# Projection tiles as four matmuls of 512 columns, and 22 steps of zero matmuls placed anew among TensorE's early steps

## The chip, the cores and the metric

One NeuronCore of a Trainium2 chip runs the whole program. The metric is the device time of one execution in microseconds (us); of the kernel before, three runs are shown and their median is the time it is compared by. A profile shows one further execution, instruction by instruction.

## The reference

The program joins two layers. The first is linear attention with exponential features, for 8 batches, 8 heads, 576 tokens and a head width of 64; the second is a gated long convolution over the 576 tokens with a model width of 512, done with Fourier transforms.

```python
def phi(x):                                   # x: (8, 8, 576, 64), w_phi: (64, 128)
    proj = np.einsum('bhsd,df->bhsf', x, w_phi)
    proj = proj - np.max(np.abs(proj), axis=-1, keepdims=True)
    return np.concatenate([np.exp(proj), np.exp(-proj)], axis=-1)
q_p, k_p = phi(q), phi(k)
kv = np.einsum('bhsf,bhsd->bhfd', k_p, v)
z = np.sum(k_p, axis=2)
x = einsum('bhsf,bhfd->bhsd', q_p, kv) / (einsum('bhsf,bhf->bhs', q_p, z)[..., None] + 1e-06)
# the heads side by side: x is (8, 576, 512)
x1, x2, x3 = split(x @ w_proj, 3)             # w_proj: (512, 1536)
x2_conv = irfft(rfft(x2) * rfft(filter))      # along the 576 tokens
out = (x1 * x2_conv * x3) @ w_out             # w_out: (512, 512)
```

## The kernel before

The order of all work is written out by hand. `PLAN` is a string of some 1,500 words; `run` takes them one after the other and calls the method of that name. A word is a step, its arguments, and behind an @ the PSUM bank (one of eight, 512 float32 columns each) in which it works; a method that needs two banks takes the next one too. Each engine executes its own steps in the order of the words; between engines there are only semaphores, which follow from who writes and reads which tile. So a step waits for the last reader of its bank and for its inputs, and everything behind it on its engine waits with it.

The 576 tokens of a batch are cut into nine residues j modulo 9 of 64 tokens. The letter b is a batch (0 to 7), v one of four pairs of heads. The steps that matter here, by engine:

- TensorE: `wz` multiplies a tile of zeros, `zz`, by itself: two matmuls of 512 columns into a bank that nothing reads (line 318). `pt` transposes q or k of batch 0 (line 613). `Qn` and `Pk` make the features of q and k with the tokens on the partitions, to find their largest absolute value (lines 639 and 632); `Qnt` and `Pkt` do so for the last residue (647). `trm` transposes the maxima (736). `Pq` makes the features of q once more, transposed, with the maximum subtracted by a second group of matmuls (666 and 672). `KV` sums k's features times v (765), `NE` multiplies q's features by that (779). `X1`, `X3` are tiles of the projection, made by `proj` (920); `X2` is its middle third, made on Fourier coefficients (898). `F` and `I` are the Fourier transform and its inverse (859, 863 and 973). `O` is the output projection (1020).
- VectorE (DVE in the profile): the reductions `maxq` and `maxk` (line 708), the division `xn` (798), products and copies from PSUM. `mlo` (732) makes the low part of the maxima.
- ScalarE (ACT): all exponentials `ex` (694), the sines of the Fourier tables (458 to 468), copies from PSUM such as `pte` (299).
- GpSimd (POOL): `vs`, which scales v (line 750), `f1` and `f2` (847, 853), and the issue of most loads.
- SyncE (SP): transposes by DMA, `trh` for q and k and `trx` for x (817), and the stores `st` (1029), in one queue.

Four things about the projection are needed. `proj` works on x transposed, `xT`, whose four blocks `kt` of 128 rows come from the four pairs of heads v and so from four separate DMA transposes. Each block holds 4 x 128 tokens, in four groups. The two halves d of the groups go through separate accumulations: for d = 0 four matmuls of 256 columns over kt = 0..3, then for d = 1 four more, which read their columns in reverse. The result is written to the bank in blocks of 128 columns, every other block for one half. There are 32 tiles of `X1` and 32 of `X3`.

Of the kernel before, what the change touches and what calls it, by code (L numbers as in the profile page):

```python
# [31 lines left out]
zeros gi_part fl_load,0,1 gz,DVE cols_i loadh,q,0,0 wz,25@2 w_load,phi loadh,k,0,1 wz,12@6  # L32
loadh,q,0,1 fl_load,3,0 wz,27@2 fl_load,3,1 cols_h gi_nr fl_load,1,1 ident cols_f gi_fr wz,20@3
fl_load,2,1 fl_load,2,0 wz,9@2 ang,2 fl_load,1,0 loadh,k,0,0 wz,10@5 fl_load,0,0 ang,3 wz,1@3
load,q,1 load,k,1 pt,q,0,0,1@7 pt,q,0,0,0@0 frac,2 pte,DVE,q,0,0,1@7 pte,ACT,q,0,0,0@0 frac,3
ang,1 sin,3 pt,k,0,1,0@5 ang,0 pt,k,0,1,1@6 w_phi sin,2 frac,1 Qn,0,0@3 cols_m pte,ACT,k,0,1,0@5
frac,0 sin,1 Pk,0,2@1 pte,DVE,k,0,1,1@6 maxk,0,2@1 pt,q,0,1,0@7 sin,0 Qn,0,1@5 one
pte,DVE,q,0,1,0@7 fa,POOL,1 maxq,0,1@5 pt,k,0,0,0@0 ex,k,p,0,2@1 pte,DVE,k,0,0,0@0 pt,k,0,0,1@5
ex,k,m,0,2@1 maxq,0,0@3 Qn,0,2@6 load,v,0 back,ACT pte,ACT,k,0,0,1@5 Pk,0,0@0 maxq,0,2@6
ex,k,m,0,0@0 trh,q,1,0 zm,POOL Pk,0,1@4 pt,q,0,1,1@3 fa,POOL,0 maxk,0,1@4 ex,k,p,0,0@0 Pk,0,3@6  # L40
trh,q,1,1 pte,ACT,q,0,1,1@3 maxk,0,0@0 ex,k,p,0,3@6 Qn,0,3@2 maxq,0,3@2 ex,k,m,0,3@6 Qnt,0@0
ex,k,p,0,1@4 maxqt,0@0 Pkt,0@2 maxk,0,3@6 mhi,0 rv@0 exkt,m,0@2 rve,ACT,0@0 trh,k,1,0 ex,k,m,0,1@4
mlo,DVE,0 maxkt,0@2 trm,0@6 rve,DVE,1@0 em,m,0,0 em,m,0,1 trme,DVE,0@6 em,p,0,0 vs,POOL,m,0,0
trh,k,1,1 Pqt,0@4 exkt,p,0@2 Qn,1,0@6 Pq,0,1@0 exqt,p,0@4 maxq,1,0@6 exqt,m,0@4 fl_loadt em,p,0,1
ex,q,m,0,1@0 Qn,1,3@6 vs,DVE,p,0,0 load,k,2 Pq,0,2@4 Pq,0,3@2 ex,q,p,0,1@0 w_load,proj,2
maxq,1,3@6 vs,POOL,p,0,1 ex,q,p,0,3@2 Pk,1,1@0 maxk,1,1@0 KV,0,0@6 ex,q,m,0,3@2 ex,q,p,0,2@4
Qnt,1@2 w_load,proj,0 KVe,DVE,0,0@6 ex,q,m,0,2@4 vs,POOL,m,0,1 maxqt,1@2 NE,0,1@6 Qn,1,2@2
ex,k,p,1,1@0 rc,0,1@6 Pq,0,0@4 xn,0,1@6 ft,ACT maxq,1,2@2 trx,0,1 KV,0,1@6 load,v,1 ex,k,m,1,1@0
load,q,2 trh,k,2,0 ex,q,p,0,0@4 Pk,1,0@0 KVe,DVE,0,1@6 w_load,proj,1 maxk,1,0@0 NE,0,2@6
ex,q,m,0,0@4 zl,POOL NE,0,3@2 rc,0,2@6 Pk,1,3@4 ex,k,p,1,0@0 xn,0,2@6 rc,0,3@2 NE,0,0@6  # L50
ex,k,m,1,0@0 xn,0,3@2 rc,0,0@6 NEt,0@2 f1,POOL,0,1,1 ex,k,p,1,3@4 xn,0,0@6 Pkt,1@0 rct,0@2
ptx,0,2@6 xnt,0,1@2 exkt,p,1@0 Hd,4@7 f1,POOL,0,0,0 xnt,0,0@2 exkt,m,1@0 ptxe,DVE,0,2@6 maxk,1,3@4
ptx,0,0@2 f1,POOL,0,1,0 He,ACT,4,0@7 Hd,0@3 ptxe,ACT,0,0@2 Qn,1,1@6 maxkt,1@0 ex,k,m,1,3@4
f1,POOL,0,0,1 Hd,3@2 maxq,1,1@6 Hd,1@0 em,m,1,0 He,ACT,0,0@3 f2,POOL,0,1,1 Pk,1,2@4 em,p,1,0
He,DVE,1,0@0 mhi,1 ptx,0,3@6 ex,k,p,1,2@4 Hd,2@7 f2,POOL,0,1,0 ptxe,DVE,0,3@6 He,DVE,0,1@3
X1,0,3@1 late He,ACT,2,0@7 maxk,1,2@4 f2,POOL,0,0,0 He,ACT,3,1@2 X1,0,2@6 He,ACT,1,1@0 mlo,DVE,1
X1,0,0@7 X1e,DVE,0,3@1 f2,POOL,0,0,1 ex,k,m,1,2@4 He,DVE,3,0@2 trm,1@3 X1e,ACT,0,0@7 trh,q,2,0
vs,DVE,m,1,0 F,0,3@4 load,v,2 trme,ACT,1@3 F,0,1@0 Fe,ACT,0,3@4 X3,0,0@2 X1e,DVE,0,2@6 em,m,1,1
vs,POOL,p,1,0 trh,k,2,1 Fe,ACT,0,1@0 F,0,2@4 tm,0,0@2 F,0,0@6 Fe,ACT,0,2@4 Pq,1,1@0 Fe,ACT,0,0@6
Pk,2,0@2 vs,POOL,m,1,1 KV,1,0@4 ex,q,p,1,1@0 maxk,2,0@2 ex,q,m,1,1@0 X2,0,3@7 KVe,DVE,1,0@4  # L60
em,p,1,1 ex,k,p,2,0@2 X3,0,2@6 vs,POOL,p,1,1 Y1,0,3@7 Xl,ACT,0 X2,0,2@1 trxt,0 ex,k,m,2,0@2
tm,0,2@6 Pk,2,1@4 Y1,0,2@1 trh,q,2,1 X2,0,0@7 load,q,3 ex,k,p,2,1@4 load,k,3 X2,0,1@3 ex,k,m,2,1@4
Y1,0,0@7 w_load,out X1,0,1@2 maxk,2,1@4 m3,POOL,0,1 Pkt,2@0 X1e,ACT,0,1@2 Pq,1,0@6 exkt,m,2@0
Y1,0,1@3 X3,0,3@2 exkt,p,2@0 ex,q,p,1,0@6 X2,0,4@5 load,k,4 maxkt,2@0 m3,POOL,0,0 tm,0,3@2 X1t,0@4
ex,q,m,1,0@6 Qn,2,1@0 Y1,0,4@5 Pq,1,2@2 em,p,2,0 em,m,2,0 maxq,2,1@0 X1te,ACT,0@4 X3t,0@7
ex,q,p,1,2@2 NE,1,1@4 vs,POOL,m,2,0 tmt,0@7 NE,1,0@0 ex,q,m,1,2@2 rc,1,1@4 xn,1,1@4 I,0,0@6
rc,1,0@0 I,0,2@4 xn,1,0@0 Ie,0,0@6 Im,0,0@6 f1,POOL,1,0,0 Pq,1,3@0 Ie,0,2@4 Ip,0,0@6 KV,1,1@2
Ip,0,2@4 ex,q,m,1,3@0 Im,0,2@4 trh,k,3,1 vs,POOL,p,2,0 ex,q,p,1,3@0 Pk,2,2@6 I,0,1@4 maxk,2,2@6
trx,1,1 KVe,ACT,1,1@2 X3,0,1@1 Ie,0,1@4 f1,DVE,1,0,1 ex,k,p,2,2@6 Ip,0,1@4 I,0,3@2 ym,POOL,0,0
Im,0,1@4 tm,0,1@1 NE,1,3@4 Ie,0,3@2 ex,k,m,2,2@6 ym,POOL,0,2 wz,13@0 Ip,0,3@2 NE,1,2@0 rc,1,3@4  # L70
Im,0,3@2 xn,1,3@4 trh,k,3,0 Pqt,1@2 ym,POOL,0,1 Qn,2,0@6 exqt,m,1@2 rc,1,2@0 KV,2,0@4 maxq,2,0@6
exqt,p,1@2 ym,POOL,0,3 trx,1,3 xn,1,2@0 NEt,1@2 KVe,ACT,2,0@4 O,0,3@6 rct,1@2 f2,DVE,1,0,0 trx,1,2
f2,DVE,1,0,1 O,0,0@7 f1,DVE,1,1,1 Oe,ACT,0,3@6 f1,DVE,1,1,0 xnt,1,1@2 Qn,2,3@4 f2,POOL,1,1,1
Qnt,2@0 xnt,1,0@2 O,0,1@6 maxq,2,3@4 O,0,2@3 Oe,ACT,0,1@6 Oe,DVE,0,0@7 F,1,0@4 f2,DVE,1,1,0
Oe,ACT,0,2@3 st,SP,0,0,1 F,1,1@6 maxqt,2@0 Fe,ACT,1,0@4 trh,q,3,1 F,1,3@2 Fe,DVE,1,1@6 F,1,2@0
Fe,ACT,1,3@2 Qn,2,2@4 Fe,ACT,1,2@0 trx,1,0 Pk,2,3@6 maxq,2,2@4 X2,1,1@3 ex,k,m,2,3@6 X2,1,2@0
trh,q,3,0 ex,k,p,2,3@6 Y1,1,1@3 X2,1,3@1 mhi,2 maxk,2,3@6 mlo,POOL,2 trh,k,4,1 load,q,4 trm,2@5
X1,1,3@2 trme,ACT,2@5 load,v,3 Y1,1,2@0 X1,1,2@4 st,SP,0,2,0 X1e,ACT,1,3@2 st,SP,0,3,1 Pq,2,1@2
Y1,1,3@1 X1e,ACT,1,2@4 Qn,3,2@6 em,m,2,1 X1,1,0@4 ex,q,p,2,1@2 maxq,3,2@6 m3,POOL,1,1 X3,1,2@5
ex,q,m,2,1@2 Pq,2,0@0 X1e,ACT,1,0@4 tm,1,2@5 Qn,3,0@6 em,p,2,1 ex,q,p,2,0@0 X3,1,0@3 vs,POOL,m,2,1  # L80
maxq,3,0@6 ex,q,m,2,0@0 NE,2,1@4 tm,1,0@3 Pq,2,2@6 Xl,ACT,1 rc,2,1@4 Pkt,3@0 X3,1,3@2 xn,2,1@4
vs,POOL,p,2,1 exkt,p,3@0 exkt,m,3@0 trx,2,1 NE,2,0@4 ex,q,p,2,2@6 tm,1,3@2 X2,1,0@3 rc,2,0@4
xn,2,0@4 trxt,1 ex,q,m,2,2@6 X1,1,1@2 Y1,1,0@3 f1,POOL,2,0,0 Pqt,2@6 trh,k,4,0 X1e,ACT,1,1@2
KV,2,1@4 maxkt,3@0 exqt,m,2@6 exqt,p,2@6 f1,DVE,2,0,1 Pk,3,1@2 st,SP,0,2,1 KVe,ACT,2,1@4 Pq,2,3@0
f2,POOL,2,0,1 maxk,3,1@2 trx,2,0 NE,2,2@6 ex,q,p,2,3@0 X2,1,4@4 m3,POOL,1,0 rc,2,2@6 ex,q,m,2,3@0
xn,2,2@6 trh,q,4,1 X1t,1@5 Y1,1,4@4 NEt,2@6 X1te,ACT,1@5 NE,2,3@0 ex,k,p,3,1@2 trx,2,2 rct,2@6
f2,POOL,2,0,0 X3,1,1@4 xnt,2,1@6 xnt,2,0@6 ex,k,m,3,1@2 rc,2,3@0 I,1,0@6 xn,2,3@0 tm,1,1@4 X3t,1@5
trx,2,3 f1,POOL,2,1,0 Ie,1,0@6 I,1,2@2 Im,1,0@6 tmt,1@5 f1,POOL,2,1,1 st,SP,0,1,1 Pk,3,0@0
Ip,1,0@6 Ie,1,2@2 Pk,3,2@4 ex,k,m,3,0@0 Ip,1,2@2 I,1,3@6 trh,q,4,0 Im,1,2@2 maxk,3,2@4 wz,14@2
ym,POOL,1,2 Ie,1,3@6 I,1,1@2 trxt,2 Im,1,3@6 ex,k,m,3,2@4 ym,POOL,1,0 Ip,1,3@6 X1,2,2@6 maxk,3,0@0  # L90
st,SP,0,0,0 X1,2,0@7 Ie,1,1@2 ex,k,p,3,2@4 st,SP,0,3,0 ym,POOL,1,3 Im,1,1@2 st,SP,0,1,0 Ip,1,1@2
X1,2,1@2 X1e,ACT,2,2@6 f2,DVE,2,1,0 X1e,ACT,2,0@7 Qn,3,3@3 X3,2,2@6 ym,POOL,1,1 em,p,3,0
maxq,3,3@3 em,m,3,0 ex,k,p,3,0@0 X1t,2@7 vs,POOL,p,3,0 tm,2,2@6 O,1,0@5 yt,ACT,1 X1te,ACT,2@7
X1e,ACT,2,1@2 Qnt,3@6 Pk,3,3@0 Oe,ACT,1,0@5 Qn,3,1@3 maxqt,3@6 ex,k,p,3,3@0 O,1,2@2 st,SP,1,0,1
maxq,3,1@3 load,q,5 F,2,0@5 ex,k,m,3,3@0 f2,POOL,2,1,1 O,1,4@7 Oe,DVE,1,2@2 Fe,ACT,2,0@5
maxk,3,3@0 O,1,3@3 load,k,5 mhi,3 Oe,ACT,1,4@7 mlo,POOL,3 F,2,1@5 load,k,6 em,m,3,1 F,2,3@0
Fe,DVE,2,1@5 vs,POOL,m,3,0 trm,3@7 X3t,2@4 Fe,ACT,2,3@0 X3,2,0@2 trme,ACT,3@7 tmt,2@4 Oe,ACT,1,3@3
F,2,2@0 tm,2,0@2 Qnt,4@4 Fe,ACT,2,2@0 Pq,3,0@6 maxqt,4@4 Qn,4,0@2 em,p,3,1 KV,3,0@0 ex,q,p,3,0@6
vs,POOL,p,3,1 maxq,4,0@2 ex,q,m,3,0@6 X2,2,2@4 KVe,ACT,3,0@0 Pq,3,1@2 vs,POOL,m,3,1 Y1,2,2@4
Pq,3,3@6 ex,q,p,3,1@2 trh,k,5,0 X2,2,3@1 ex,q,m,3,1@2 NE,3,0@4 Y1,2,3@1 load,v,4 st,SP,1,2,1  # L100
X3,2,1@0 ex,q,p,3,3@6 st,SP,1,2,0 rc,3,0@4 Pq,3,2@2 ex,q,m,3,3@6 m3,POOL,2,1 xn,3,0@4 X2,2,0@1
tm,2,1@0 trx,3,0 ex,q,p,3,2@2 NE,3,1@4 Y1,2,0@1 X2,2,1@7 ex,q,m,3,2@2 X1,2,3@6 rc,3,1@4 Xl,DVE,2
xn,3,1@4 Y1,2,1@7 Qn,4,2@2 X1e,ACT,2,3@6 trx,3,1 Pkt,4@0 KV,3,1@4 maxkt,4@0 m3,POOL,2,0 X3,2,3@6
# [982 lines left out]
```

## Time and profile before

| | |
|---|---|
| three runs | 307.57, 308.5, 310.66 us; median 308.5 us |
| the profiled execution | 307.3 us, of which 305.5 us from the first to the last instruction |
| TensorE's mean granted clock in the span | 0.969 |
| TensorE busy | 275.5 us, 4253 matmuls, 4287 weight loads |
| VectorE, ScalarE, GpSimd busy | 262.3, 223.0 and 216.4 us |

In the profile's rows the first number is the start in us from the span's start, the second the time that the row takes, then the engine, the line of the kernel, the operation, what it writes and reads, its shape and how many instructions are merged. The bracket at the end is the idle time of that engine before the row and what ended it. A matmul's length holds its way through the array: matmuls follow one another more closely than their lengths say, so their pitch is read from the starts of two rows.

### The profile page before, as it was taken

The numbers are of one execution on the slowest core, as the hardware profiler recorded it, in microseconds if no ns is written. First come the engines' busy times: TensorE is split into PE (matmuls) and PEld (weight loads), VectorE is DVE, ScalarE is ACT, GpSimd is POOL, SyncE is SP. The second block draws the span as 40 slices with busy tenths as digits, with TensorE's granted clock in tenths as the row PEclk, the third lists the DMA queues.
The fourth block names the chain that finished last, engine by engine and source line by source line (L and its number), as shares of the span: only waits on it lengthen the run. The fifth ranks groups of instructions, "written<-read, shape, count | busy, mean of one in ns | idle before, by whom it ended". The sixth has DMA issues, their size and how long they took to land.

```text
span 305.5 us, 10146 instructions
## 1 busy us (share of the span) xinstructions
PE 275.5 (90%) x4253; PEld 199.7 (65%) x4287; DVE 262.3 (86%) x448; ACT 223.0 (73%) x360; POOL 216.4 (71%) x180
## 2 busy tenths in 40 slices
...
ACT  1998986888359978876987688976757988843240
...
PEclk9855999999999999999999999999999999999998
...
GB/s 144 242 200 133 206 136 179 157 153 191 108 118 187 144 136 134 189 177 144 131 151 154 140 92 177 165 163 102 4 139 65 103 89 10 72 55 60 2 120 190
DMA packets 72734, 40.18 MB, mean 132 GB/s; under 512 B 53040, under 2 KB 67504, under 8 KB 72688
## 3 DMA queue, kind: packets, MB, share of 16 engines
...
q14 instruction: 13, 0.11, 0.1%
HBM read 33.75 MB, written 9.44 MB: 141 GB/s over the span
## 4 chain that ended last, share of the span: by engine, by line
PE 69%; DVE 15%; ACT 5%; DMA 5%; issue 4%; SPq 0%; DVEq 0%
PE ps L920 15%; PE ps L898 9%; PE ps L1020 8%; PE ps L973 6%; PE ps L765 5%; DMA xT<-xn 5%; PE ps L779 3%; DVE mk L708 3%; PE ps L666 3%; PE ps L929 2%; PE ps L672 2%; PE ps L639 2%; PE ps L859 2%; PE ps L318 2%; PE ps L863 2%
## 5 line engine op out<-in xcount | busy, mean ns | idle before, releaser
L920 PE MATMUL ps<-xT,wproj 128*128 128x256 bf16 x512 | 64.2, 273 | 2.3 <-DMA xT<-xn 2.2
L920 PEld LDWEIGHTS <-wproj 128*128 128x128 bf16 x512 | 48.3, 98 | 12.7 <-issue 2.9
L708 DVE TENSOR_REDUCE mk<-ps 128x8 f32<-128x1024 f32 (+1 forms) x40 | 44.2, 1109 | 6.1 <-PE ps L632 5.4
L708 DVE TENSOR_REDUCE mq<-ps 128x8 f32<-128x1024 f32 (+1 forms) x40 | 44.0, 1109 | 5.1 <-PE ps L639 3.6
L912 POOL TENSOR_TENSOR T<-T,T 128x1024 bf16<-128x1024 bf16 x15 | 31.9, 2127 | 18.3 <-DVE T L908 18.2
L1009 POOL TENSOR_TENSOR yT<-cv,x1s 128x576 bf16<-128x576 f32 x27 | 34.3, 1295 | 11.6 <-DVE cv L994 11.5
L750 POOL TENSOR_TENSOR vm<-vn,vm 128x1152 bf16<-128x1152 bf16 x15 | 32.9, 2194 | 9.3 <-ACT vm L744 9.3
L694 ACT ACTIVATE Ekp<-ps 128x1024 bf16<-128x1024 f32 x32 | 33.1, 1033 | 3.9 <-PE ps L632 2.6
L694 ACT ACTIVATE Ekm<-ps 128x1024 bf16<-128x1024 f32 x32 | 33.0, 1032 | 4.0 <-DVE mk L708 2.6
L750 POOL TENSOR_TENSOR vp<-vn,vp 128x1152 bf16<-128x1152 bf16 x15 | 32.2, 2155 | 5.1 <-ACT vp L744 5.1
L694 ACT ACTIVATE Eqp<-ps 128x1024 bf16<-128x1024 f32 x32 | 32.8, 1026 | 3.4 <-PE ps L672 3.2
L1020 PE MATMUL ps<-wout,yT 128*128 128x512 bf16 x130 | 34.0, 380 | 1.2 <-DVE yT L1009 0.4
L694 ACT ACTIVATE Eqm<-ps 128x1024 bf16<-128x1024 f32 x32 | 32.5, 1028 | 3.3 <-PE ps L672 2.5
L847 POOL TENSOR_TENSOR SD<-xn 128x512 bf16<-128x512 bf16 x23 | 26.3, 1160 | 10.1 <-DVE xn L798 8.6
L853 POOL TENSOR_TENSOR xf<-SD 128x512 bf16<-128x512 bf16 x24 | 27.8, 1169 | 7.1 <-DVE SD L847 5.7
L898 PE MATMUL ps<-wproj,XF 128*128 128x512 bf16 x116 | 30.3, 380 | 0.9 <-ACT XF L299 0.2
L973 PE MATMUL ps<-inv,T 128*128 128x288 bf16 x192 | 27.6, 286 | 0.1
L994 DVE TENSOR_TENSOR cv<-es,ps 128x288 f32<-128x288 f32 x64 | 25.6, 443 | 1.4 <-ACT es L991 1.1
L299 ACT CAST x1s<-ps 128x512 bf16<-128x512 f32 (+1 forms) x34 | 17.9, 543 | 11.8 <-PE ps L920 9.9
L961 DVE TENSOR_TENSOR x1s<-ps,x1s 128x512 bf16<-128x512 f32 x32 | 21.7, 684 | 5.0 <-PE ps L920 4.1
L991 ACT COPY es<-ps 128x288 f32<-128x288 f32 x32 | 12.9, 404 | 14.2 <-PE ps L973 13.7
L798 DVE TENSOR_TENSOR xn<-ps,r 128x512 bf16<-128x512 f32 x32 | 22.0, 689 | 0.9
...
## 6 DMA issues: line engine op xcount, KB each, us to landing
...
```

Source lines behind the costliest of these rows:

```text
L694: self.nc.scalar.activation(e, p, AF.Exp, bias=0.0, scale=1.0 if g == "p" else -1.0)
L708: self.nc.vector.tensor_reduce(out=out, in_=src, axis=AX.X, op=ALU.max, apply_absolute_value=True)
L750: self.eng(eng).tensor_tensor(out=t[:, :, :, 0:64], in0=self.at("vn", b)[:, 2 * X:2 * X + 2], in1=t[:, :, :, 64:65].to_broadcast([128, 2, ...
L847: self.eng(eng).tensor_tensor(out=o[:, :, 2 * i:2 * i + 2, :], in0=x[:, :, 0:2, :], in1=x[:, :, 2:4, :], op=ALU.subtract if i else ALU.add)
L853: self.eng(eng).tensor_tensor(out=o[:, :, 2 * i:2 * i + 2, :], in0=x[:, :, 0:4:2, :], in1=x[:, :, 1:4:2, :], op=ALU.subtract if i else ALU ...
L898: self.mm(self.pb(0), l, w[:, kt, 512:1024], start=(kt == 0), stop=(kt == 3))
L912: self.eng(eng).tensor_tensor(out=Y, in0=Y, in1=self.at(f"T{2 * e + 1}", b), op=ALU.add)
L920: self.mm(o[:, d], w[:, kt, f0 + 128 * m:f0 + 128 * m + 128], y[:, 1, ::-1, ::-1] if d else y[:, 0], start=(kt == 0), stop=(kt == 3))
L973: self.mm(self.pb(e, 0, 288), l, inv[:, 2 * e + i if i < 2 else 4 + e, :], start=(i == 0), stop=(i == 2))
L994: self.nc.vector.tensor_tensor(out=self.turn_of("cv", (b, m))[:, :, odd, :], in0=self.turn_of("es", (b, m)).rearrange("p (x t) -> p x t", ...
L1009: self.eng(eng).tensor_tensor(out=self.at("yT", b)[:, m, 0:SEQ], in0=self.turn_of("cv", (b, m)).rearrange("p x h t -> p (x h t)"), in1=sel ...
L1020: self.mm(self.pb(0), y[:, kt, 128 * c:128 * c + 128], w[:, kt, :], start=(kt == 0), stop=(kt == 3))
```

## The change

Three edits belong together. First, `proj` makes a tile with four matmuls of 512 columns, one for each kt, and no longer with two halves. Second, so that the columns stand in the right order without a reversed reading, the token order of two of the four groups is turned at its sources: in the choice of the feature slice in `NE`, in the choice of the stationary slice in `F`, in the table of token numbers `nr` for the inverse transform, and in the rows that a store writes. Third, `PLAN` has 22 words `wz` where it had ten. Some methods that no word calls (`Ft`, `Fs`, `It`, `Is`) are gone.

```diff
     def proj(self, b, f0, m):
         w, x = self.at("wproj"), self.at("xT", b)
-        o = self.pb(0).rearrange("p (g d x) -> p d g x", g=2, d=2)
-        for d in range(2):
-            for kt in range(4):
-                y = x[:, kt].rearrange("p (g d) x -> p d g x", g=2)
-                self.mm(o[:, d], w[:, kt, f0 + 128 * m:f0 + 128 * m + 128],
-                        y[:, 1, ::-1, ::-1] if d else y[:, 0], start=(kt == 0),
-                        stop=(kt == 3))
+        for kt in range(4):
+            self.mm(self.pb(0), w[:, kt, f0 + 128 * m:f0 + 128 * m + 128],
+                    x[:, kt].rearrange("p a x -> p (a x)"), start=(kt == 0), stop=(kt == 3))
...
-                    y = 2 * (1 - u if a % 2 else u) + a // 2
-                    E = self.turn_of("Eq" + g, (b, v))[:, y, a % 2, :]
+                    g, d = a // 2, a % 2
+                    y = 2 * (1 - u) + 1 - g if d else 2 * u + g
+                    E = self.turn_of("Eq" + sg, (b, v))[:, y, d, :]
...
-                self.mm(self.pb(e, 144 * s, 144 * s + 144), xf[:, v, 2 * s + e, :],
+                self.mm(self.pb(e, 144 * s, 144 * s + 144), xf[:, v, 2 * (1 - s) + 1 if e else 2 * s, :],
...
-        g.iota(self.nr[:, 0:256], pattern=[[5, 2], [1, 4], [9, 32]], base=1,
-               channel_multiplier=0, **IOTA)
+        for d in range(2):
+            z = 1 - 2 * d
+            g.iota(self.nr[:, 128 * d:128 * d + 128], pattern=[[z, 4], [9 * z, 32]],
+                   base=288 if d else 1, channel_multiplier=0, **IOTA)
...
-        bb, j = (b, (0, 2, 5, 7)[c] + i) if c < 4 else (b - 1 + i, 4)
+        bb, j = (b, (0, 2, 8, 6)[c] + (-i if c > 1 else i)) if c < 4 else (b - 1 + i, 4)
+        dst = self.out[bb][j:SEQ:9, :]
+        if c in (2, 3):
+            dst = dst.rearrange("(h t) d -> h t d", h=2)[:, ::-1, :]
```

Apart from `wz`, the words of `PLAN` are the same, and so is their order on TensorE, VectorE, GpSimd and SyncE; on ScalarE one pair of neighbours changes places (`back` and `pte,ACT,k,0,0,1`). Of the ten `wz` before, seven stood ahead of everything else on TensorE, and one each at about 75, 110 and 141 us of the profile. Of the 22 after, six stand ahead of everything, fifteen are spread between the transposes, `Qn`, `Pk` and `Pq` of batch 0, and one stands where that at 75 us stood.

The first place is on TensorE, between the transposes of q and the first ones of k (`qn` and `kn` are the loaded q and k, `zz` the zeros). Before:

```order
L613 LDWEIGHTS qn_75
L613 MATMUL ps<-ident_63,qn_75 128x128
L613 LDWEIGHTS kn_77
L613 MATMUL ps<-ident_63,kn_77 128x128
L613 LDWEIGHTS kn_77
```

After:

```order
L617 LDWEIGHTS qn_75
L617 MATMUL ps<-ident_63,qn_75 128x128
L320 LDWEIGHTS zz_74
L320 MATMUL ps<-zz_74 128x512
L320 LDWEIGHTS zz_74
L320 MATMUL ps<-zz_74 128x512
```

Three steps of zeros, six matmuls, now stand where the transposes of k followed at once.

The second place is on TensorE, between the subtraction of the maxima in `Pq,0,1` (`mT` and `one`) and `Qn,1,3` (`qT` and `wphi`). Before:

```order
L672 MATMUL ps<-mT_91,one_64 128x4x32
L639 LDWEIGHTS qT_82
L639 MATMUL ps<-wphi_62,qT_82 128x128
L639 LDWEIGHTS qT_82
L639 MATMUL ps<-wphi_62,qT_82 128x128
```

After:

```order
L676 MATMUL ps<-mT_91,one_64 128x4x32
L320 LDWEIGHTS zz_74
L320 MATMUL ps<-zz_74 128x512
L320 LDWEIGHTS zz_74
L320 MATMUL ps<-zz_74 128x512
L320 LDWEIGHTS zz_74
L320 MATMUL ps<-zz_74 128x512
L320 LDWEIGHTS zz_74
L320 MATMUL ps<-zz_74 128x512
L643 LDWEIGHTS qT_82
L643 MATMUL ps<-wphi_62,qT_82 128x128
```

Two steps of zeros, four matmuls, have come between them. Ten more steps stand in the same way: one each before `Pk,0,3`, `Qn,0,3`, `Qnt,0`, `Pkt,0` and `trm,0`, and five at four places between the first transposes of k and `Qn,0,2`.

250 lines of the change are left out of this document (113 added, 137 removed).

## The prediction, on record before the changed kernel ran

> **What bounds the kernel now.** I read the totals first (the table above), then ScalarE's busy share and TensorE's clock in 40 slices, then the chain of work that ended last.
>
> ```profile
> ACT  1998986888359978876987688976757988843240
> PEclk9855999999999999999999999999999999999998
> PE 69%; DVE 15%; ACT 5%; DMA 5%; issue 4%; SPq 0%; DVEq 0%
> ```
>
> TensorE carries 69% of the chain and is busy for 275.5 of 305.5 us; but slices 2 to 4, of 7.6 us each, have less than the full clock, and in them ScalarE is busy for eight or nine tenths. The early stage, the only one that the zeros can help, has its own limit. Its stretches of 3.4 us, between the times at which the granted clock changed (busy time of TensorE, instructions, clock, DMA):
>
> ```profile
> 6.78:10.19 3.41, 1.70 (x24) 1.00 1.15 271
> 10.19:13.61 3.42, 1.43 (x31) 1.00 1.19 235
> 13.61:17.02 3.41, 0.82 (x8) 0.50 1.21 207
> 27.26:30.67 3.41, 2.95 (x52) 0.50 0.58 83
> 30.67:34.08 3.41, 2.55 (x100) 1.00 1.21 205
> 51.20:54.60 3.40, 1.93 (x20) 1.00 1.24 155
> ```
>
> After two stretches with 50% and 42% busy the clock was halved, from 13.6 to 30.7 us; a stretch with 57% later on did not halve it. Who waits for the slow matmuls there, by order of time:
>
> ```profile
> 1.34 5.87 PE L318 MATMUL ps<-zz 128*128 128x512 bf16 x14 [1.34 <-DVE zz L313]
> 7.04 0.67 PE L613 MATMUL ps<-ident,qn 128*128 128x128 bf16 x9
> 7.74 0.69 ACT L299 COPY qT<-ps 128x640 bf16<-128x640 bf16 x1 [5.72 <-PE ps L613]
> 28.43 1.02 ACT L694 ACTIVATE Eqp<-ps 128x1024 bf16<-128x1024 f32 x1
> 30.28 1.02 ACT L694 ACTIVATE Eqp<-ps 128x1024 bf16<-128x1024 f32 x1 [0.83 <-PE ps L672]
> ```
>
> ScalarE waits 5.72 us for the first transposes, which stand behind 14 zero matmuls; from 7.74 us to the end of the row at 28.43 it has hardly a gap, and then it waits 0.83 us for `Pq,0,3`. Between those two waits ScalarE is the limit, and a faster TensorE is worth nothing there.
>
> **The change, part by part.** (1) *The start.* Twelve zero matmuls stand in front in place of 14. Fourteen took from 1.34 to 7.04 us, 0.407 each, of which only the last ones ran at the full clock, so twelve end near 6.4 us. The first transposes move up by some 0.6 us if q has landed (they show no wait for it at 7.04, no row says how much earlier it was there); those nine would then run partly at half clock, which takes about 0.15 back (0.67 us for nine at the full clock, up to twice the pitch for the first few). I take -0.45 for ScalarE's start, from 0 to -0.6.
>
> (2) *The clock.* With zeros in the gaps, the halving at 13.6 should not come. The worth is ScalarE's wait of 0.83. It ends when `Pq,0,3` is made, after `Qn,1,3` and `Pq,0,2`:
>
> ```profile
> 27.02 0.45 PE L672 MATMUL ps<-mT,one 64*128 64x128 bf16 x4
> 27.92 0.61 PE L639 MATMUL ps<-wphi,qT 64*128 64x128 bf16 x8 [0.46 <-DVE mq L708]
> 28.30 0.45 PE L666 MATMUL ps<-qT,wphi 64*128 64x256 bf16 x2
> 29.80 0.45 PE L672 MATMUL ps<-mT,one 64*128 64x128 bf16 x4
> 34.10 0.29 PE L666 MATMUL ps<-qT,wphi 64*128 64x256 bf16 x2 [0.29 <-ACT Eqm L694]
> 34.43 0.29 PE L672 MATMUL ps<-mT,one 64*128 64x128 bf16 x4
> ```
>
> (The first row is the end of `Pq,0,1`, ahead of it.) At half clock this ran from 27.92 to 30.25, two `Pq` taking 28.30 to 30.25. At the full clock the four parts of one `Pq` follow each other by 0.11 (34.10 to 34.43 is three of them), 0.44 in all, so the two take 0.88 and a tail of 0.2, and `Qn` 0.2, half of the 0.38 before 28.30: about 1.25 in place of 2.33. The 1.08 saved are more than the 0.83, so the wait goes. The next to be late is `KV,0,1`, whose second product needs GpSimd's scaled v:
>
> ```profile
> 32.27 2.16 POOL L750 TENSOR_TENSOR vm<-vn,vm 128x1152 bf16<-128x1152 bf16 x1
> 34.83 0.43 PE L765 MATMUL ps<-vm,Ekm 64*128 64x65 bf16 x16
> 36.54 0.24 PE L765 MATMUL ps<-vp,Ekp 64*128 64x65 bf16 x4 [1.06 <-issue]
> ```
>
> It ends at 34.43 and is read at 34.83: 0.40 of room. GpSimd works in its own order behind ScalarE's first part, so it moves up with the start alone, 0.45. Parts 1 and 2 together are therefore worth 0.45 + 0.40 = 0.85 at `KV,0,1`, not 0.45 + 0.83. Right after it TensorE stood 1.06 us for its own instructions in the middle of a step. The extra steps move the place in the instruction stream, so this stall may go, stay, or come elsewhere: 0 taken, from -1.06 to +1.06.
>
> What do the zeros cost? At the full clock a matmul of 512 columns has a pitch of 0.22 (rows below), a step 0.43. Four of them stand ahead of `Qn,1,3`, which waited until 27.92 for a reduction while `Pq,0,1` was done: 0.87 us into a gap that the full clock widens, so nothing. The steps ahead of `Qnt`, `Pkt`, `trm` and `Pk,0,3` each work in the bank of the step that they delay and wait for the same reader, so these come 0.43 later, less what their own matmuls gain; ScalarE and VectorE, which read the results, have other work queued (8 and 9 tenths busy, above). Where that cover is gone it is 0.43 each.
>
> (3) *Projection tiles.* A tile of eight matmuls stands next to a group of four of 512 columns in one place, all back to back:
>
> ```profile
> 216.59 1.04 PE L920 MATMUL ps<-xT,wproj 128*128 128x256 bf16 x8
> 217.46 1.03 PE L898 MATMUL ps<-wproj,XL 128*128 128x512 bf16 x4
> 218.33 1.04 PE L920 MATMUL ps<-xT,wproj 128*128 128x256 bf16 x8
> ```
>
> From start to start 0.87 and 0.87: the columns set the time, and the halved number of instructions and weight loads is hidden by them. So 64 tiles give 0, within the 0.01 of the rows: from -0.6 to +0.6. [...]
>
> The new order within a tile does matter where a tile waits for the last DMA transpose of x. Three tiles stop before their block kt = 3, or kt = 1 in the third:
>
> ```profile
> 141.25 4.13 DMA xT<-xn
> 144.25 0.50 PE L920 MATMUL ps<-xT,wproj 128*128 128x256 bf16 x3
> 145.42 1.58 PE L920 MATMUL ps<-xT,wproj 128*128 128x256 bf16 x13 [0.67 <-DMA xT<-xn]
> 176.53 0.49 PE L920 MATMUL ps<-xT,wproj 128*128 128x256 bf16 x3
> 177.29 1.58 PE L920 MATMUL ps<-xT,wproj 128*128 128x256 bf16 x13 [0.28 <-DMA xT<-xn]
> 275.73 1.29 PE L920 MATMUL ps<-xT,wproj 128*128 128x256 bf16 x8
> ```
>
> Before, three matmuls of 256 columns ran ahead of the wait and five behind it; now three of 512 run ahead and one behind, so 3 x 0.11 = 0.33 more is done in the idle time. There is 0.67 and 0.28 of it: -0.33 and -0.28. The third takes 1.29 instead of 1.04 and has one matmul ahead: -0.11. The chain of waits passes through the first (the row of 4.13 us), so I count all: -0.72, from 0 to -0.72.
>
> (4) *Late zeros.* Two pairs are gone.
>
> ```profile
> 110.32 0.38 PE L318 MATMUL ps<-zz 128*128 128x512 bf16 x1
> 110.75 0.90 PE L973 MATMUL ps<-inv,T 128*128 128x288 bf16 x6
> 141.24 0.59 PE L318 MATMUL ps<-zz 128*128 128x512 bf16 x2
> ```
>
> The first pair delays `I,1,1` by 0.43 with no idle time around it: -0.43. The second stands before the wait at 145.42, which grows by as much: 0.
>
> (5) *The rest.* `NE` and `F` only read other slices of the same size: 0. Half the stores name two blocks of 32 rows. Their issue on SyncE's queue costs 0.51 for a plain one, and 0.52 for each of seven loads with a more divided pattern:
>
> ```profile
> 84.40 0.51 SPq L1029 DMA_DIRECT2D out_dram<-o  x1
> 2.44 3.65 SPq L476 DMA_DIRECT2D fl<-in_moe_filter_fft_dram  x7
> ```
>
> So 0, though each 0.1 more would stand ahead of the transposes in that queue.
>
> The sum: -0.85 - 0.72 - 0.43 = -2.0, to 305.3 us from the profiled execution's 307.3. That execution was 1.2 under the median of the three runs, so the forecast against the median of 308.5 is **306.5**.
>
> **The rivals.** *The clock falls all the same* (slower). Filled by the new steps, the stretch from 10.2 to 13.6 has 1.43 + 0.43 of 3.4 busy, 55%, and the next about as much: between the 50% and 42% that halved the clock and the 57% that kept it. Then a step of zeros takes 0.87 (double the pitch) on TensorE ahead of work that is waited for. Its place is `Qn,1,3`: four zeros behind `Pq,0,1`, whose row ends at 27.47, run to 29.2 in place of 27.92, +1.25. Of the nine other steps from `Pk,0,2` to `trm` I count two, +1.7, since ScalarE has hardly a gap in which to hide them (none to all nine are the bounds). That is +2.95 - 0.45 - 0.72 - 0.43 = +1.35, 309.9 on the median. It decides if the clock is below 1 at 27 us. For it: the shares lie at the edge. Against: at half clock the zeros double the busy share, and 86% brought the clock back at 30.7.
>
> The longest idle time of TensorE ahead of the halving is two thirds of such a stretch:
>
> ```profile
> 12.48 0.40 PE L632 MATMUL ps<-wphi,kT 64*128 64x128 bf16 x8 [1.99 <-ACT kT L299]
> ```
>
> [...]
>
> *More than the sum.* The stall of 1.06 goes, and so does another at the end of the early stage:
>
> ```profile
> 49.66 2.96 DVE L732 TENSOR_TENSOR mh<-mq,mh 128x36 bf16<-128x36 f32 x1
> 52.67 0.23 PE L736 MATMUL ps<-ident,mh 128*128 128x128 bf16 x1 [2.23 <-DVE mh L732]
> ```
>
> A tiny product took 2.96 us on VectorE, and TensorE waited 2.23 for it; if the shift frees either one, the gain is 3.0 to 5.2, 303.3 to 305.4 on the median. Against: VectorE and GpSimd both move by the same 0.85, so what they meet in stays.
>
> *Nothing arrives.* The late waits for xT follow chains that end on VectorE, and the early gain is lost at 50 us in the same stall, if it ends at a fixed time: 308.3.
>
> **How the numbers follow.** Forecast 0.50, more 0.27, clock falls 0.13, nothing 0.10. The range, 302.8 to 310.0, takes in the gain with one stall gone and the slower rival's time, and leaves out both stalls gone at once and a clock lost for longer. About 1% (3.1 us) is what a measurement of this kernel tells from no change. Faster by more, under 305.4, is all of "more" and, through part 2's stall and a spread of 1.2 between execution and median, some 0.3 of the forecast: 0.42. Slower by more, over 311.6, is half of the slower rival: 0.06. The rest is 0.52.
>
> **What would show it.** The clock at 1.00 in all slices from 7 us on; ScalarE's first copy near 7.3; no wait before the second `Eqp`; 256 matmuls on line 906 with a pitch of 0.22; the waits for xT at the two late places shorter by about 0.3. I am wrong if the clock still halves, if tiles get cheaper by more than 0.01, or if VectorE's row of 2.96 us changes by more than all of this.

## The result, and the profile after

The changed kernel takes **352.12 us** (median of six executions, 348.18 to 360.93) against 309.58 for the kernel before, timed beside it (six, 307.57 to 315.31). The ratio is 1.135, with an interval of 1.125 to 1.145. Medians here and below are over all executions; ratios leave out those more than some 1.5% above the fastest of their kernel, and where too few were left no ratio is given.

The page of the changed kernel: busy time and instructions of each engine, TensorE's clock and the share of the DMA engines in 40 slices, then the chain of work that ended last, by engine and by line.

```profile
PE 285.8 (82%) x4055; PEld 177.8 (51%) x4055; DVE 265.9 (76%) x448; ACT 223.3 (64%) x360; POOL 217.6 (62%) x181
PEclk9897699999999999999999998999969999999955
DMA  7999999399899989986997999970936404500323
PE 48%; DMA 27%; DVE 14%; issue 4%; ACT 2%; SPq 2%; POOL 1%; DVEq 0%; ACTq 0%; POOLq 0%
DMA out_dram<-o 12%; PE ps L906 10%; PE ps L887 7%; DMA qT<-qn 6%; PE ps L991 5%; PE ps L769 4%; PE ps L958 4%; DMA xT<-xn 4%; DMA qn<-in_q_dram 3%; DVE mk L712 3%; PE ps L784 2%; PE ps L670 2%; PE ps L914 2%; PE ps L864 2%; DMA xTt<-xnt 2%
```

The engines do hardly more than before (TensorE 285.8 us against 275.5, VectorE 265.9 against 262.3), and the clock is lower in few slices. What is new is in the chain: DMA has 27% of it where it had 5%, and the largest part, 12%, is the landing of stores, which the chain of before does not name at all. The long pieces of that chain, by start and length in us:

```profile
104.31 6.18 DMA xTt<-xnt
121.51 5.92 DMA out_dram<-o
...
202.24 17.30 DMA out_dram<-o
...
244.83 11.50 DMA qT<-qn
...
321.00 7.33 DMA out_dram<-o
329.05 12.31 DMA out_dram<-o
```

The store instructions of the two kernels (shortest, median and longest issue in ns, then first and last start), before and after, and from the list of waits of each (us in all, times, longest): copies into `o`, the four buffers from which the stores read, that waited for a store to leave its buffer, and TensorE's waits for a transpose:

```profile
L1029 SPq DMA_DIRECT2D out_dram<-o x67: 466/587/1538, 84.4 to 301.2; - x67
...
PE ps L920 <- DMA xT<-xn: 2.2, 3, 1.2
...
ACT o L299 <- DMA out_dram<-o: 1.1, 1, 1.1
```

```profile
L1003 SPq DMA_DIRECT2D out_dram<-o x67: 466/550/2962, 88.9 to 342.2; - x67
...
DVE o L303 <- DMA out_dram<-o: 15.3, 4, 11.4
ACT o L301 <- DMA out_dram<-o: 7.8, 3, 3.4
PE ps L643 <- DMA qT<-qn: 7.4, 2, 6.0
PE ps L906 <- DMA xT<-xn: 6.4, 5, 2.3
```

The issue of a store costs what it did. The first store goes out at 88.9 instead of 84.4 us, and from there to the end of the span it takes 260.8 us (349.7 - 88.9) instead of 221.1 (305.5 - 84.4). So **39.7 of the 44.2 us come after the first store.**

The trace also holds every update of a store's completion semaphore. A store of 64 plain rows has 16; in the kernel before, the last one comes 2.5 us after the issue at the median. A turned store, of two blocks of 32 rows (32 of the 72 stores are such), has 3: the first at about 1 us, the last at a median of 7.3 us and at worst at 17.3. Transfers beside them land later too, though nothing in them was changed: the stores that stayed plain went from 2.6 to 4.9 us at the median (those on SP's queue), the DMA transposes of q from 4.2 to 6.3, and from 10.2 to 23.6 at worst. For the transposes of k only the worst grew, from 16.9 to 24.2; their median fell from 6.7 to 5.8.

### The profile page after: what moved, and what is told of

The parts are those of the page before. It is cut to its first block, busy times and chain, and to the rows that moved or that the text cites. A ratio compares the mean times of both kernels' runs of the same rounds, so it can differ in the third digit from the quotient of the medians.

```text
span 349.7 us, 9715 instructions
## 1 busy us (share of the span) xinstructions
PE 285.8 (82%) x4055; PEld 177.8 (51%) x4055; DVE 265.9 (76%) x448; ACT 223.3 (64%) x360; POOL 217.6 (62%) x181
## 4 chain that ended last, share of the span: by engine, by line
PE 48%; DMA 27%; DVE 14%; issue 4%; ACT 2%; SPq 2%; POOL 1%; DVEq 0%; ACTq 0%; POOLq 0%
DMA out_dram<-o 12%; PE ps L906 10%; PE ps L887 7%; DMA qT<-qn 6%; PE ps L991 5%; PE ps L769 4%; PE ps L958 4%; DMA xT<-xn 4%; DMA qn<-in_q_dram 3%; DVE mk L712 3%; PE ps L784 2%; PE ps L670 2%; PE ps L914 2%; PE ps L864 2%; DMA xTt<-xnt 2%
## 5 line engine op out<-in xcount | busy, mean ns | idle before, releaser
L906 PE MATMUL ps<-xT,wproj 128*128 128x512 bf16 x256 | 63.8, 379 | 6.7 <-DMA xT<-xn 6.4
L906 PEld LDWEIGHTS <-wproj 128*128 128x128 bf16 x256 | 23.2, 97 | 31.9 <-issue 7.6
L754 POOL TENSOR_TENSOR vm<-vn,vm 128x1152 bf16<-128x1152 bf16 x15 | 34.0, 2269 | 7.5 <-ACT Fkp L701 5.3
L852 POOL TENSOR_TENSOR SD<-xn 128x512 bf16<-128x512 bf16 x23 | 26.3, 1159 | 15.3 <-DVE xn L803 13.8
L991 PE MATMUL ps<-wout,yT 128*128 128x512 bf16 x144 | 35.4, 380 | 0.4 <-DVE yT L980 0.4
L887 PE MATMUL ps<-wproj,XF 128*128 128x512 bf16 x128 | 31.3, 380 | 0.2 <-ACT XF L301 0.2
L784 PE MATMUL ps<-KVs,Eqm 128*128 128x65 bf16 x256 | 20.8, 198 | 4.9 <-issue 4.9
```

Source lines behind the costliest of these rows:

```text
L754: self.eng(eng).tensor_tensor(out=t[:, :, :, 0:64], in0=self.at("vn", b)[:, 2 * X:2 * X + 2], in1=t[:, :, :, 64:65].to_broadcast([128, 2, ...
L784: self.mm(self.pb(u, 65 * a, 65 * a + 65), E, KVs[:, u, v, s, :], start=(s == 0), stop=(s == 1))
L852: self.eng(eng).tensor_tensor(out=o[:, :, 2 * i:2 * i + 2, :], in0=x[:, :, 0:2, :], in1=x[:, :, 2:4, :], op=ALU.subtract if i else ALU.add)
L887: self.mm(self.pb(0), l, w[:, kt, 512:1024], start=(kt == 0), stop=(kt == 3))
L906: self.mm(self.pb(0), w[:, kt, f0 + 128 * m:f0 + 128 * m + 128], x[:, kt].rearrange("p a x -> p (a x)"), start=(kt == 0), stop=(kt == 3))
L991: self.mm(self.pb(0), y[:, kt, 128 * c:128 * c + 128], w[:, kt, :], start=(kt == 0), stop=(kt == 3))
```

## The experiments

**Theory S**: a turned store is carried by as many DMA engines as it has outer blocks, two, and these are overfilled. **Theory C**: the zeros, the clock and an early stall on VectorE set off a chain that the stores only show. **Theory P**: the four wide matmuls read xT in a way that delays it. **Rival R**: the descending row step costs, not the number of blocks.

**e1, plain stores in the changed kernel.**

```diff
-        if c in (2, 3):
-            dst = dst.rearrange("(h t) d -> h t d", h=2)[:, ::-1, :]
```

> The changed kernel with every store written as 64 rows in order, so the rows of the chunks c = 2 and 3 go to other places within their 64 rows; all work is done. Theory S (the stores of two blocks of 32 turned rows cost the time, because each is carried by a few DMA engines only: 3 completion updates against 16 for a plain store): all that came after the first store goes, and what is left is the 4.5 us that the first store is late (88.87 against 84.40) less what the new order of the projection gives: 309 to 315 us, median landing of a store near the 2.5 us of before, o waits for out_dram gone. Theory C (the zeros and the clock: the early stall at DVE's v.p product and the halved clock set off a chain that the stores only show): 340 us or more. Theory P (four matmuls of 512 columns read xT in a way that delays it): 340 us or more.

312.83 us (median of 4, 305.69 to 317.63) against 310.96 for the kernel before beside it (7, 308.48 to 314.37). With these two lines gone, so is the loss: the medians differ by 1.9 us, which four executions 12 us apart do not tell from nothing. C and P fall.

**e2, turned stores in the kernel before.**

```diff
+        dst = self.out[bb][j:SEQ:9, :]
+        if c in (2, 3):
+            dst = dst.rearrange("(h t) d -> h t d", h=2)[:, ::-1, :]
...
-            out=self.out[bb][j:SEQ:9, :], in_=o[64 * i:64 * i + 64, :])
+            out=dst, in_=o[64 * i:64 * i + 64, :])
```

> The kernel before with nothing changed but the form of the stores of chunks 2 and 3: two blocks of 32 rows, turned, as in the change; those rows land in other places within their 64 rows. Theory S: slower by 30 to 45 us, 338 to 355 us, with landings of 7 us and more and o waiting for out_dram. Theories C and P: 307 to 310 us, nothing moves.

359.94 us, ratio 1.153 (1.142 to 1.164): the same loss and a little more, without the new zeros, without the new tiles; S had 355 at most. Its waits show the same picture:

```profile
DVE o L301 <- DMA out_dram<-o: 14.7, 4, 9.3
PE ps L920 <- DMA xT<-xn: 9.2, 5, 3.3
```

**e3, e10 and e4, the number of blocks**: the changed kernel with 4, 8 and 16 blocks (one number in the line).

```diff
-            dst = dst.rearrange("(h t) d -> h t d", h=2)[:, ::-1, :]
+            dst = dst.rearrange("(h t) d -> h t d", h=4)[:, ::-1, :]    # e3; 8 in e10, 16 in e4
```

> The changed kernel with the turned stores cut as four blocks of 16 rows, each turned (rows land in other places within their 64 rows). Theory S, by the count of the outer blocks: twice the engines, so half the landing time, 315 to 335 us. Rival R (the turned row step costs, not the number of blocks): as the changed kernel, 348 to 353 us. Theories C and P: 348 to 353 us.

> The changed kernel with the turned stores cut as eight blocks of 8 rows (rows land in other places within their 64 rows). Theory S: nine completion updates, a median landing of about 3.1 us (the medians of 32, 16 and 4 rows per engine, 7.1, 4.7 and 2.4 us, lie on 1.8 us and 0.165 us a row), 42 us of load on each of the eight engines, which the stage hides: 310 to 319 us. Rival (the time follows the landing in proportion): 322 to 328 us.

> The changed kernel with the turned stores cut as sixteen blocks of 4 rows, each turned (rows land in other places within their 64 rows). Theory S, by the count of the outer blocks: 16 engines share each store as they do a plain one, so the time of the plain stores within 1 per cent, 309 to 316 us, median landing about 2.5 us. Rival R (the turned row step costs): 348 to 353 us. Theories C and P: 348 to 353 us.

329.34 us (4 executions) with four blocks, 313.94 (10; ratio 0.995, 0.988 to 1.002) with eight, 314.26 (4) with sixteen. With 16 blocks the rows of each block still step backwards, and nothing is lost: R falls. One thing these kernels do not separate: the length of a backward run of rows is in each the number of rows that an engine would carry. No run has two blocks of rows in rising order; what speaks for the engines is the number of updates below. The stores on SP's queue (issue in ns, first and last start in us) with two blocks in the kernel before (e2), then with four, eight and sixteen blocks, and plain (e1):

```profile
L1032 SPq DMA_DIRECT2D out_dram<-o x67: 466/550/2249, 88.5 to 353.2; - x67
```

```profile
L1003 SPq DMA_DIRECT2D out_dram<-o x67: 466/571/2249, 90.8 to 326.6; - x67
```

```profile
L1003 SPq DMA_DIRECT2D out_dram<-o x67: 466/598/1277, 87.5 to 305.8; - x67
```

```profile
L1003 SPq DMA_DIRECT2D out_dram<-o x67: 466/587/1365, 90.4 to 308.8; - x67
```

```profile
L1001 SPq DMA_DIRECT2D out_dram<-o x67: 466/587/1467, 90.8 to 311.6; - x67
```

| store | updates recorded | median landing of those on SP | span less first store |
|---|---|---|---|
| two blocks, changed kernel | 3 | 7.28 us | 349.7 - 88.9 = 260.8 us |
| two blocks, kernel before (e2) | 3 | 7.06 | 359.7 - 88.5 = 271.2 |
| four (e3) | 5 | 4.67 | 332.6 - 90.8 = 241.8 |
| eight (e10) | 9 | 2.93 | 310.2 - 87.5 = 222.7 |
| sixteen (e4) | 16 | 2.41 | 313.1 - 90.4 = 222.7 |
| plain (e1) | 16 | 2.49 | 315.9 - 90.8 = 225.1 |
| plain, kernel before | 16 | 2.51 | 305.5 - 84.4 = 221.1 |

(Landings of the turned stores; of all stores in the plain rows. The profiled executions of e1 and e3, 317.63 and 334.35 us, are some 5 us over their medians, so their last column is too long by about as much.) The stage before the first store lasts 84 to 91 us in all of them, with no order in it: e2 has the early code of before, and 88.5.

In these stores the updates are the number of blocks plus one, up to 16: 2 + 1, 4 + 1, 8 + 1, and 16 with sixteen blocks as with 64 plain rows; the extra one comes at about 1 us. That each of the others stands for one DMA engine is the author's reading, and theory S rests on it: no run here shows how many engines carried a store, or which ones.

How much is too much can be estimated, if that reading holds and each engine has one block to carry (4 rows of a plain store). From 4 to 32 rows an engine the median landing grows from 2.41 to 7.06 us, 0.166 a row, but a median can hold waiting behind other transfers (one and the same plain form lands in 2.2 to 10.5 us in the kernel before). The shortest landings of the turned stores should hold the least of it: 2.26 us with sixteen blocks (2.22 for the plain stores of the kernel before), then 2.69, 3.53 and 5.12 with two. They lie on a line of (5.12 - 2.26) / 28 = 0.102 us a row. If the two engines are always the same, the 32 turned stores put 32 x 32 x 0.102 = 104 us on each (170 by the medians), in a stage of 221 us, in which each engine has this to do in the kernel before (length of the stretch, then busy time and instructions of TensorE, its weight loads, VectorE, ScalarE and GpSimd, then the clock, the mean share of the DMA engines and GB/s):

```profile
84.40:90.00 5.60, 4.85 (x48) 2.93 (x47) 5.03 (x7) 4.18 (x8) 1.00 (x2) 1.00 0.89 118
90.00:150.00 60.00, 58.22 (x948) 44.86 (x957) 52.08 (x82) 48.52 (x79) 50.02 (x38) 1.00 0.99 157
150.00:200.00 50.00, 48.69 (x855) 35.40 (x859) 44.40 (x67) 41.24 (x65) 44.45 (x32) 1.00 1.00 146
200.00:250.00 50.00, 47.99 (x703) 34.79 (x707) 44.90 (x74) 37.35 (x63) 33.77 (x25) 1.00 0.48 91
250.00:305.50 55.50, 49.26 (x630) 35.28 (x633) 41.79 (x69) 26.32 (x46) 26.69 (x18) 0.98 0.32 74
```

That is 5.0 + 59.4 + 50.0 + 24.0 + 17.8 = 156 us, 13 of them for these stores in plain form (4 rows an engine; 21 by the medians). Two blocks: 156 - 13 + 104 = 247 us (305 by the medians), more than 221 either way. Four: 195 (220). Eight: 169 (178), and sixteen 156, with room. The shares are of packets' times, which overlap (the share was 1.21 in before from 13.61 to 17.02 us), so this is an estimate of where the edge lies and not of the time. It puts two blocks over the edge; four, which cost some 17 us against e1, it does not explain, unless the stretches from 90 to 200 us count alone, where the engines are at 0.99 and 1.00 already.

**e9, six buffers for `o` instead of four**, to tell a full queue from a late single landing.

```diff
-... 'r': 4, 'o': 4, 'kn': 2, ...
+... 'r': 4, 'o': 6, 'kn': 2, ...
```

> The changed kernel with six buffers for o instead of four, nothing else. Theory Q (the turned stores fill the two engines that carry them: 32 stores of 7.1 us each are 226 us of a stage that lasts 221 us in the kernel before, so everything else on these engines, the transposes too, stands in line): no gain, 346 to 354 us, since a deeper ring only lengthens the line. Theory B (the single late landing costs, through the copies that wait for a free o, 23 us of waits on DVE and ScalarE in the changed kernel's trace): 325 to 340 us.

355.25 us, ratio 1.137 (1.128 to 1.145). The copies' wait for a free buffer fell from 23.1 (15.3 + 7.8) to 10.9 us, and nothing was gained.

```profile
DVE o L303 <- DMA out_dram<-o: 10.9, 2, 10.2
```

So B falls: the latency that the ring of buffers has to cover is not what is short. Q is what is left, the capacity of two engines, and the plain stores that landed at 4.9 us instead of 2.6 speak for it. That a plain store shares the two engines with the turned ones, and ends only when these are through with its part, is the author's reading of this; no trace here tells one engine from another.

**e5 to e8, the other parts alone**, in one comparison (12 executions each; the kernel before 311.75, 35 executions, 308.15 to 316.9). e5 is before with the new list of steps; e6 is e5 with one word of the list moved; e7 exchanges two loops, so that a tile is one accumulation instead of two; e8 is the new projection and token order with the old list and plain stores.

```diff
-... em,p,0,0 vs,POOL,m,0,0 ... ex,q,m,0,1@0 vs,DVE,p,0,0 Qn,1,3@6 ...        # e6 against e5
+... em,p,0,0 vs,DVE,p,0,0 vs,POOL,m,0,0 ... ex,q,m,0,1@0 Qn,1,3@6 ...
...
-        for d in range(2):                                                  # e7 against before
-            for kt in range(4):
...
+        for kt in range(4):
...
+            for d in range(2):
...
-                        y[:, 1, ::-1, ::-1] if d else y[:, 0], start=(kt == 0),
-                        stop=(kt == 3))
+                        y[:, 1, ::-1, ::-1] if d else y[:, 0], start=(kt == d == 0),
+                        stop=(kt == 3 and d == 1))
```

> The kernel before with the change's list of steps alone: its twelve more steps of zeros and their places, and the projection, layout and stores as before. Theory L (the early loss is the lock between DVE and GpSimd: DVE's v.p product, ready after GpSimd has begun to issue the load of k for batch 2, waits until GpSimd is through with its run, 5.3 us against 1.35): slower than before by 2 to 5 us, first store at 88 to 91 us, a v.p product of 5 us where GpSimd was first. Theory Z (the zeros hold the clock and bring what was forecast, 0.4 to 2 us; the late first store of the other kernels comes from the projection and the layout): 0.4 to 2 us faster than before, first store at 82 to 84 us.

> The kernel of the zeros alone with one step moved: DVE's v.p product stands right behind the weights it needs (ScalarE had them at 24.6 us in the changed kernel, DVE was idle from 24.4 to 26.6), ahead of the maximum of q of batch 1. Theory L: the product takes 1.4 us, TensorE's wait of 4.8 us behind it goes, 3 to 4.5 us below the zeros alone, first store 3 us sooner or more. Theory Z: no change against the zeros alone within 1 us.

> The kernel before with the two loops of the projection exchanged: kt outside, the two halves of 256 columns inside, eight matmuls as before; so the tile's last quarter of xT is needed by the last two matmuls instead of the fourth and the eighth. The forecast's term: 0.7 us faster, from the three waits for xT. Rival: within 0.3 us of before, since what follows waits in their place, or the clock's changes bury it.

> The changed projection of four matmuls of 512 columns with its layout of xn, xf and inv, but before's list of steps (no more zeros) and plain stores, so the rows of the chunks c = 2 and 3 go to other places within their 64 rows. The forecast: the tiles cost the same (0.87 us by both pitches), the order of kt brings 0.7, so 0.7 us faster than before, first store at 84 us. Rival (the other way of the early loss): the layout or the projection makes the first store 2 to 6 us late, 1 to 4 us slower than before.

| | median | ratio, interval |
|---|---|---|
| e5, zeros alone | 313.89 us | 0.997, 0.991 to 1.004 |
| e6, v.p product first | 313.59 | 1.004, 0.999 to 1.008 |
| e7, kt outside | 312.34 | 0.997, 0.992 to 1.002 |
| e8, projection alone | 309.71 | 0.993, 0.989 to 0.998 |

e5 and e7 cannot be told from the kernel before; e5's ratio is just under 1, its median over all executions 0.7% above. e8 is 0.7% faster, about 2 us, though the execution that was traced took 314.14 us and has its first store at 90.05 us, not at the 84 that was expected.

In e5 the clock did hold better (a mean of 0.978 over its executions against 0.957). The 14 traces of this case show what the list does to it. In all six kernels with the old list (before, e2, e7, e8, e11, e12) the clock is halved between 10.9 and 13.7 us, for 17 to 31 us. With the new list this happens by 14 us in three of eight (the changed kernel, e1, e6), for 3.4 to 6.8 us; in the other five the first halving comes at 26.8 us or later. In e5's trace `KV,0,1` starts at 32.63 us, 1.9 sooner than in that of before (34.54). Then TensorE stood in two gaps that the profile marks issue, which means that it waited for nothing that the profile shows:

```profile
34.47 0.40 PE L767 MATMUL ps<-vm,Ekm 64*128 64x65 bf16 x14 [1.22 <-issue]
...
42.86 0.58 PE L829 MATMUL ps<-ident,xn 128*128 128x128 bf16 x4 [2.67 <-issue]
```

All such gaps of TensorE add up to 7.6 us in this trace and to 2.9 in that of before. Over the traces whose stores cost nothing they are 2.9 to 5.1 us with the old list (before, e7, e8, e11, e12) and 4.2 to 10.2 with the new one (e1, e4, e5, e6, e10). What they may be the traces suggest: each gap above 1 us in these two ends 2.2 to 2.4 us after a packet of 16 KB of instructions (queue 8) began to load, at 34.35 us in before and at 32.03, 40.49 and 195.18 in e5. That the gain went there fits; no run took the stalls away, so it is not shown.

e6 was aimed at the early stall of the changed kernel. VectorE's product took 5.29 us there (1.35 before), and TensorE waited 4.78 for what stood behind it:

```profile
27.22 0.80 POOL L595 DMA_DIRECT2D kn<-in_k_dram  x1
27.70 5.29 DVE L754 TENSOR_TENSOR vp<-vn,vp 128x1152 bf16<-128x1152 bf16 x1
28.02 0.75 POOL L585 DMA_DIRECT2D wproj<-in_moe_w_proj_dram  x1
28.77 2.17 POOL L754 TENSOR_TENSOR vp<-vn,vp 128x1152 bf16<-128x1152 bf16 x1
30.87 0.80 POOL L585 DMA_DIRECT2D wproj<-in_moe_w_proj_dram  x1
31.69 3.29 POOL L754 TENSOR_TENSOR vm<-vn,vm 128x1152 bf16<-128x1152 bf16 x1
...
34.17 0.62 PE L769 MATMUL ps<-vp,Ekp 64*128 64x65 bf16 x16 [4.78 <-DVE mq L712]
```

Moved forward, it met GpSimd's product of v.m, which had begun 0.16 us sooner, and took 3.20:

```profile
26.43 2.15 POOL L752 TENSOR_TENSOR vm<-vn,vm 128x1152 bf16<-128x1152 bf16 x1 [7.23 <-ACT vm L746]
26.59 3.20 DVE L752 TENSOR_TENSOR vp<-vn,vp 128x1152 bf16<-128x1152 bf16 x1 [0.20 <-ACT vp L746]
```

The forecast of 3 to 4.5 us for e6 failed, partly because e5's profiled execution did not have the long product (1.66 us). The product took 5.07 to 5.40 us in four of the 14 traces (the changed kernel, e3, e4 and e8, which has the old list) and 1.35 to 1.67 in nine. In the changed kernel GpSimd had begun 0.48 us before it (27.22 and 27.70); in before the two begin together (27.79) and it takes 1.35. That the order of the starts decides is the author's reading. With either list there are long ones and short ones, so it is no mark of the change.

**e12, the small product of batch 1 (`mlo`) on GpSimd.**

```diff
-... maxk,1,2@4 f2,POOL,0,0,0 He,ACT,3,1@2 X1,0,2@6 He,ACT,1,1@0 mlo,DVE,1
+... maxk,1,2@4 f2,POOL,0,0,0 He,ACT,3,1@2 X1,0,2@6 He,ACT,1,1@0 mlo,POOL,1
```

> The kernel before with one small product of batch 1, the low part of the maxima of q, on GpSimd instead of DVE, where it took 2.96 us at 49.66 us with 36 columns a partition. Theory L (it waited for the port that GpSimd held through the load of v and the v.p product): DVE's wait goes, 1 to 2.9 us faster. Rival: DVE's next product of the same kind, v.m of batch 1, takes over the wait for GpSimd, and the time stays within 0.7 us.

313.79 us against 312.1, ratio 1.008 (1.004 to 1.012): slower by 0.4 to 1.2%, where L had it faster and the rival within 0.7 us. The trace has what the rival named: `mlo` shrank to 0.24 us on GpSimd, and VectorE's next product of the same kind took over its wait and more, 5.16 us instead of 1.34. That this is the whole loss is not shown.

```profile
48.80 0.24 POOL L732 TENSOR_TENSOR mh<-mq,mh 128x36 bf16<-128x36 f32 x1
...
50.90 2.17 POOL L750 TENSOR_TENSOR vp<-vn,vp 128x1152 bf16<-128x1152 bf16 x1
51.24 5.16 DVE L750 TENSOR_TENSOR vm<-vn,vm 128x1152 bf16<-128x1152 bf16 x1
53.02 2.16 POOL L750 TENSOR_TENSOR vm<-vn,vm 128x1152 bf16<-128x1152 bf16 x1
```

**e11, the projection with its rows put right**, for a version that keeps what e8 gained. The tiles of y are made in two parts, the second turned, and residue 4 is carried turned until there.

```diff
...
+        self.eng(eng).tensor_tensor(out=o[:, 0:8], in0=cv[:, 0:8], in1=x[:, 0:8], op=ALU.mult)
+        self.eng(eng).tensor_tensor(out=o[:, 8:18, ::-1], in0=cv[:, 8:18], in1=x[:, 8:18],
+                                    op=ALU.mult)
...
```

> The projection alone with its rows put right on the chip: the product y is made in two instructions a tile instead of one, the second writes its blocks of 32 columns turned, and the rows of chunk 4 are carried turned until there; the stores are plain, the list of steps is that of before. Theory: GpSimd has the time for 27 more short instructions, so the time is that of the projection alone, 0 to 1.2 per cent below before. Rival: y is waited for by the output projection and GpSimd's second instruction makes it late, or the two stretch DVE's: 1 to 2 per cent above before.

311.0 us (12, 308.94 to 314.34) against 312.1 (29), ratio 0.9955 (0.992 to 0.999). **This version is 0.1 to 0.8% faster than the kernel before**, and so far ahead of the changed one. The two parts on GpSimd cost 672 and 792 ns where one took 1282, 27 times 0.18 us more on that engine:

```profile
L982 POOL TENSOR_TENSOR yT<-cv,x1s x27: 663/672/853, 75.6 to 297.8; 128x256 bf16<-128x256 f32 x27
L983 POOL TENSOR_TENSOR yT<-cv,x1s x27: 782/792/801, 76.2 to 298.4; 128x320 bf16<-128x320 f32 x27
```

## Why the prediction was wrong, step by step

**The step that failed is (5), the rest**: "Half the stores name two blocks of 32 rows. Their issue on SyncE's queue costs 0.51 ... So 0". The issue does cost that, but the step priced only the instruction that starts the transfer and put the transfer itself at nothing, without a row for a transfer of two blocks. Its nearest row was a load with a divided pattern whose outer dimension is still 32, and so could not show what an outer dimension of 2 does. (The turned stores are 32 of 72, not half.) The term was about 40 us (39.7 behind the first store in the profiled executions; 39.3 between the medians of the changed kernel and e1; 49.0 from before to e2). None of the rivals contained it. The eight loads of `fl` on SyncE's queue have 16 completion updates each in the trace of before, the turned stores 3 in that of the changed kernel; no row of before shows what a transfer with so few costs.

The other steps, by their own numbers:

1. *The start*: forecast -0.45 us. ScalarE's first copy began at 6.38 instead of 7.74 (first row below), -1.36, three times as much. But these are two executions. Over the traces the copy begins at 6.56 to 7.78 us with 14 zero matmuls in front (six kernels, median 7.39) and at 6.38 to 7.54 with twelve (eight, median 6.94): the medians differ by 0.45, as forecast. Much of the spread is the time at which the clock first rises to full, 4.08 to 6.85 us in the six, in the same order as their copies.

```profile
6.38 0.69 ACT L301 COPY qT<-ps 128x640 bf16<-128x640 bf16 x1 [4.36 <-PE ps L617]
29.18 1.02 ACT L698 ACTIVATE Eqp<-ps 128x1024 bf16<-128x1024 f32 x1 [0.24 <-PE ps L676]
```

2. *The clock*: the sign of being wrong that the prediction named, a clock that still halves, came in part. In the changed kernel's trace it was halved at 10.87 us for 3.4 us and at 31.35 for 10.2; at 27 us it was full, so the rival that rests on a halved clock there is not what happened. The wait of 0.83 before the second `Eqp` shrank to 0.24 (second row above) and went in e5. What that brought at `KV,0,1`, 0.85 by the forecast, is open: where VectorE's product before it was short, `KV,0,1` starts at 32.63, 34.43, 34.76 and 35.46 us with the new list (e5, e10, e9, e1) and at 34.54 to 35.20 with the old (before, e12, e7, e2, e11); e5's 1.9 is the best of four. Nothing of it reached the end. Of "0 taken, from -1.06 to +1.06" for the instruction stall the width was too small: 1.22 remained in e5 and 2.67 came in another place. In the changed kernel's trace the gain ended at VectorE's product of 5.29 us, a place that the prediction does not name; the second halving came while TensorE stood behind it (columns as in the stretches above):

```profile
10.19:13.61 3.42, 2.65 (x29) 1.44 (x23) 2.46 (x6) 3.42 (x6) 0.00 (x0) 0.60 1.18 241
30.67:34.08 3.41, 0.00 (x0) 0.00 (x0) 3.41 (x3) 2.28 (x3) 3.39 (x3) 0.60 1.09 188
```

3. *The tiles*: same pitch, as forecast (0.86 and 0.87 between the starts):

```profile
236.11 1.03 PE L906 MATMUL ps<-xT,wproj 128*128 128x512 bf16 x4
236.97 1.03 PE L887 MATMUL ps<-wproj,XL 128*128 128x512 bf16 x4
237.84 0.38 PE L906 MATMUL ps<-xT,wproj 128*128 128x512 bf16 x1
```

The order of kt alone (e7) gives -0.3%, with an interval that holds both the forecast 0.72 us and nothing. e8's 2 us (0.8 to 3.4) may be more than the 0.72; which part of it brings the rest is open. The waits for xT that the term counted are 2.2, 2.0, 2.4 and 0.9 us with the old tiles (before, e5, e12, e6), 2.0 in e7 and 0.6 to 1.8 with the new tiles where the stores cost nothing (e8, e11, e10, e4, e1): one trace of each does not settle it.

4. *Late zeros*: -0.43 is too small to be told apart here.

With stores that cost nothing the change is worth nothing that can be measured (e1's median within 1% of before; eight blocks 0.995, 0.988 to 1.002). The sum of -2.0 us, 0.6%, lies in that interval, and so does 0: these runs neither bear it out nor refute it.
